# Leaky relu through an SBUF tile in six of nine chunks, one transfer for two heads' decay rows, and stores issued by ScalarE

## The chip, the cores and the metric

The kernel runs on one core of a Trainium2 chip. A core has a matrix engine (TensorE, PE in the profile; PEld is its weight load), a vector engine (VectorE, DVE), an activation engine (ScalarE, ACT), a general engine (GpSimd, POOL), and a sequencer that here issues every transfer (SyncE, SP; SPq in the rows). Each works through its own list of instructions in the order written at build time, and waits at an instruction until what it needs is there. The metric is the device time of one execution in microseconds, as the median of three runs.

## The reference, cut to what matters

```python
scores = q @ k.T / sqrt(D)                         # 4 batches x 8 heads, 576 x 576, D = 64
scores = where(causal, -1e9, scores + cum[i] - cum[j])   # cum: running sum of log(clip(f))
x   = softmax(scores) @ v                          # to 2304 tokens x 512
g   = maximum(0.01 * h, h);  h = x @ w_in          # 512 -> 2048
x   = g @ w_out                                    # 2048 -> 512
h   = x @ w_in2                                    # 512 -> 1024
ln  = layernorm(h * softmax(h)) * g_ln
out = ln @ w_out2                                  # 1024 -> 512
```

## The kernel before, in words

Every product is made with two parts per operand: a rounded high part and the rest (low part), and three matmuls high-high, high-low, low-high. So whatever feeds a matmul has first to be split by one copy (high) and one subtraction (low).

Attention runs over 16 pairs of heads in eight passes (`PASSES`, two per batch): an A pass makes query blocks 0 and 1 of four pairs, a B pass blocks 2, 3 and 4. For an A pass `prep_full` loads keys and queries into a `raw` tile of 64 rows and puts under them four rows of decay, which it reads from a DRAM tensor `dr_d` (for the first batch they lie in `qa` from the start). For a B pass `prep_split` loads a `raw` tile and splits it into `kq` tiles. Scores go to PSUM (`ps_s`), through the masked maximum (L707) and the exponential (L657) to a 16-bit tile `hl`; SP turns that with a DMA transpose into `pt` (L470), PE multiplies it with the values into `ps_v`, and `evac` brings the result into a tile `xr` (L739 on ACT, L742 on DVE). When a pair is done, `pair` stores `xr` to a DRAM tensor `xs_d`.

The first half of the feed-forward part, `ffn_a`, takes nine blocks of 256 tokens in the order `ORDER` = (0, 1, 4, 2, 5, 3, 6, 7, 8). Block n below 8 is batch n mod 4, tokens 0 to 255 or 256 to 511, so that a block can start only when a whole pass of its batch is stored: `load_x` reads the block back from `xs_d` into tiles `sd` and splits it into tiles `x`. Then `hidden` does nine of the sixteen chunks of 128 hidden columns: 12 matmuls into a PSUM tile `ps_f` (three of these exist), the leaky relu twice on ACT (L853 rounds it into the high part of `g`, L854 writes it back to PSUM), and on DVE the difference of the two as the low part (L855). The nine `g` tiles then make four partial outputs y (`ps_f<-g,wo`, 27 matmuls each), which are copied to `yo` tiles and stored to the DRAM tensor `yp_d`. The `yo` tiles are two of their own and two halves of an `sd` tile, so that rows name them either way. The tiles `x` and `g` lie where the weights were staged, so that no block starts before all 18 pieces of first-half weights are converted. Later `ffn_b` does the other seven chunks and adds the partial y back, and `layer2` does the rest.

What stands where in each engine's list is not written out by hand. Every operation is given to a planner (`Plan`) with a priority, a list of engines that may do it and a duration on each (`flex`); the planner runs through a model of the engines and puts each operation on an engine when its inputs are there and a buffer is free. So an edit at one place can move instructions everywhere. `move` takes the engines that may issue a transfer; its default is `QUEUES = ("SP",)`, and no caller names another.

Of the kernel before, what the change touches and what calls it, by code (L numbers as in the profile page):

```python
# [7 lines left out]
F32 = mybir.dt.float32  # L8
# [5 lines left out]
AF = mybir.ActivationFunctionType  # L14
# [10 lines left out]
FA = 9  # L25
PT = 4
NVT = 8
NRAW = 3
NWST = 3
NE = 2  # L30
# [327 lines left out]
def body(tc, kqa, kq, vt, f, wa, w2i, w2o, gln, out):  # L358
# [107 lines left out]
    def load(buf, dst, src, nbytes, prio, mode="w", **kw):  # L466
        return move(dst, src, nbytes, prio, **{mode: [buf]}, **kw)
# [30 lines left out]
    def row(h, p):  # L498

        return KD * h + p if p < KD else 2 * KD + (NP - KD) * h + p - KD  # L500
# [65 lines left out]
    def prep_full(p, prio):  # L566


        if p < KD:
            bq = QA[0]  # L570
            QK[p] = [[(bq, p), (bq, "n"), (bq, "c")]] * 2, lambda hd: qa[0:66, hd, p], {0: 256, 1: 384}
            return
        bq = P.buf("raw")
        a = lambda r0, r1: bq.t[r0:r1, 0:1024].rearrange("r (h c) -> r h c", h=2)
        load((bq, 0), lambda: a(0, 64), lambda: kqa[p].rearrange("(h d) c -> d h c", h=2), 64 * 1024 * 4, prio - LD)
        for hd in range(2):
            for c0, k0 in ((0, 0), (256, KB)):
                load((bq, (hd, c0)), lambda hd=hd, c0=c0: a(64, 68)[:, hd, c0:c0 + 256], lambda hd=hd, k0=k0: dr_d[row(hd, p), :, k0:k0 + 256], 4096, prio - LD,
                     deps=st["cols"])
        QK[p] = [[bq]] * 2, lambda hd: a(0, 68)[:, hd], {0: 256, 1: 384}  # L580

    def prep_split(p, prio):
# [196 lines left out]
    def pair(p, prio, blocks):  # L779
        n0 = len(P.ops)  # L780
        b, kd = divmod(p, KD)
        full = len(blocks) == 2
        (prep_full if full else prep_split)(p, prio)
        if 0 in blocks:
            prep_v(p, prio)
        xr = P.buf("xr")
        k = 0
        for hd in range(2):
            pts = {}
            for unit in UNITS[len(blocks)]:  # L790
                pts.update(scores(p, unit, hd, prio + SM + KSTEP * k, full))
                k += 1
            pv(p, hd, pts, xr, prio + AV)
            if hd == HD4 and 4 in blocks:
                pv4(p, scores4(p, prio + SM + KSTEP * k, full), xr, prio + AV)
                k += 1
        c0, c1 = 128 * blocks[0], min(S, 128 * blocks[-1] + 128)
        o = move(lambda: xs_d[b][:, kd, c0:c1], lambda: xr.t[:, c0:c1], 128 * (c1 - c0) * 4, prio - 400, r=[xr])
        spills.append((b, c0, c1, o))
        attn_ops.extend(P.ops[n0:])  # L800

# [33 lines left out]
        weight(w2o[c], W2O[c], prio, scale=lambda: glt[:, c:c + 1])  # L835


    def hidden(c, xb, n, pst, gt, prio, eprio):
        ps, g = P.buf(pst), P.buf(gt)
        w = WI[c]  # L840

        def pe():
            for k in range(KD):
                wh, wl = (w.t[:, j, 128 * k:128 * k + 128] for j in range(2))
                xh, xl = (xb[k].t[:, j, 0:n] for j in range(2))
                o = ps.t[:, 0:n]
                mm(o, wh, xh, k == 0, False)
                mm(o, wh, xl, False, False)
                mm(o, wl, xh, False, k == KD - 1)

        P.op(PE, 12 * mmr(n), pe, prio, w=[ps, (g, "slot")], r=xb + [w])
        h = lambda: ps.t[:, 0:n]
        P.op(ACT, act(n, 0, True), lambda: nc.scalar.activation(g.t[:, 0, 0:n], h(), AF.Prelu, scale=WSC, alpha=0.01), eprio, w=[(g, 0)], r=[ps])  # L853
        P.op(ACT, act(n, 0, True), lambda: nc.scalar.activation(h(), h(), AF.Prelu, scale=WSC, alpha=0.01), eprio, rw=[ps])  # L854
        P.op(DVE, dve(n) + 60, lambda: nc.vector.tensor_tensor(  # L855
            g.t[:, 1, 0:n], h(), g.t[:, 0, 0:n].bitcast(F32), op=ALU.subtract), eprio, w=[(g, 1)], r=[ps, (g, 0)])
        return g
# [33 lines left out]
    def ffn_a(blk, prio):  # L891
        eprio = prio - EP
        xb = load_x(blk, prio, "x")
        gs = [hidden(c, xb, TB, "ps_f", "g", prio + c, eprio + c) for c in range(FA)]
        YPD[blk] = []
        for d in range(KD):
            ps, yo = P.buf("ps_f"), P.buf("yo")
            for q in range(2):
                cs = range(FA // 2 * q, FA if q else FA // 2)

                def pe(cs=cs, d=d, ps=ps):
                    for c in cs:
                        y_mms(ps.t[:, 0:TB], c, d, gs[c], TB, c == 0, c == FA - 1)

                P.op(PE, 3 * len(cs) * mmr(TB), pe, prio + EPD + d, r=[gs[c] for c in cs] + [WO[c] for c in cs],
                     **({"w": [ps]} if q == 0 else {"rw": [ps]}))
            copy_f(lambda yo=yo: yo.t, lambda ps=ps: ps.t[:, 0:TB], TB, eprio + EPD + d, engs=(ACT, DVE), scale=lambda: WSC * WSC, psum=True, w=[yo], r=[ps])
            YPD[blk].append(move(lambda d=d: yp_d[blk][:, d], lambda yo=yo: yo.t, 128 * TB * 4, prio - 3000, r=[yo]))

    def ffn_b(tb, prio):  # L910
        eprio, blk = prio - 3000, ORDER[tb]
# [233 lines left out]
```

## Time and profile before

| | |
|---|---|
| runs | 846.91, 848.83, 849.77 us; median 848.83 |
| profiled execution | 848.65 us, its span 846.9 us |
| PE busy | 767.9 us, 91% |
| DVE, ACT, POOL busy | 519.4, 490.1, 348.8 us (61%, 58%, 41%) |
| DMA | 108.37 MB, mean 128 GB/s |
| chain that ended last | PE 64%, DMA 10%, DVE 9%, ACT 8% |

The shares are averages over stages that differ. The matmuls of block 0 begin at 92.4 us. From there to 391.1 us attention and `ffn_a` share PE, from 391.1 to 455.5 us `ffn_a` has PE alone, and from then on the second half runs. Busy time of PE is the time in which a matmul is under way.

### The profile page before, as it was taken

The numbers are of one execution on the slowest core, as the hardware profiler recorded it, in microseconds if no ns is written. First come the engines' busy times: TensorE is split into PE (matmuls) and PEld (weight loads), VectorE is DVE, ScalarE is ACT, GpSimd is POOL, SyncE is SP. The second block draws the span as 40 slices with busy tenths as digits, with TensorE's granted clock in tenths as the row PEclk, the third lists the DMA queues.
The fourth block names the chain that finished last, engine by engine and source line by source line (L and its number), as shares of the span: only waits on it lengthen the run. The fifth ranks groups of instructions, "written<-read, shape, count | busy, mean of one in ns | idle before, by whom it ended". The sixth has DMA issues, their size and how long they took to land.

```text
span 846.9 us, 16019 instructions
## 1 busy us (share of the span) xinstructions
PE 767.9 (91%) x5648; PEld 695.5 (82%) x5648; DVE 519.4 (61%) x1350; ACT 490.1 (58%) x1242; POOL 348.8 (41%) x448
## 2 busy tenths in 40 slices
PE   1753798979999999999899998999999999999996
PEld 1432698968998999999899987898889988998885
DVE  5788767888888878884654667334633434253551
ACT  4886768889889889884555543232333243333321
POOL 6648545166618564822610443422332233222321
PEclk9999999989999999999999999999999999999999
DMA  8997457687789677694655643321332131312223
GB/s 230 220 223 245 96 130 151 150 221 154 136 162 216 155 163 151 174 160 148 195 172 177 189 104 104 71 79 16 98 71 68 26 87 38 87 26 63 26 56 82
DMA packets 184402, 108.37 MB, mean 128 GB/s; under 512 B 150033, under 2 KB 167137, under 8 KB 184321
## 3 DMA queue, kind: packets, MB, share of 16 engines
q1 hardware_dynamic: 184320, 107.35, 52.3%
q8 instruction: 44, 0.72, 0.4%
q14 instruction: 38, 0.30, 0.1%
HBM read 57.39 MB, written 14.78 MB: 85 GB/s over the span
## 4 chain that ended last, share of the span: by engine, by line
PE 64%; DMA 10%; DVE 9%; ACT 8%; issue 4%; POOL 3%; SPq 0%; ACTq 0%; DVEq 0%; POOLq 0%
PE ps_f L473 40%; PE ph L473 10%; PE py L473 6%; PE ps_s L473 5%; PE ps_v L473 3%; ACT ps_s L657 2%; DMA raw<-w2o 2%; DMA tr<-hl 2%; DMA raw<-kq 2%; DMA wst<-wa 1%; DMA pt<-hl 1%; ACT hl L427 1%; DVE hl L438 1%; DMA qa<-sd 1%; DVE ps_s L707 1%
## 5 line engine op out<-in xcount | busy, mean ns | idle before, releaser
L473 PE MATMUL ps_f<-x,wi 128*128 128x256 f32 x972 | 131.7, 289 | 1.2 <-POOL x L442 1.1
L473 PE MATMUL ps_f<-g,wo 128*128 128x256 f32 x972 | 126.4, 284 | 2.5 <-DVE g L855 2.5
L473 PEld LDWEIGHTS ps_f<-x,wi 128*128 128x128 f32 x972 | 124.7, 193 | 3.1 <-POOL x L442 1.9
L473 PEld LDWEIGHTS ps_f<-g,wo 128*128 128x128 f32 x972 | 120.8, 188 | 4.0 <-DVE g L855 2.9
L473 PE MATMUL ph<-wi,g 128*128 128x512 f32 x408 | 98.5, 397 | 1.4 <-DVE raw L968 1.4
L473 PE MATMUL ps_f<-x,wib 128*128 128x256 f32 x756 | 97.3, 279 | 1.8 <-DVE g L855 1.7
L438 DVE SCALAR_TENSOR_TENSOR hl<-ps_s,st,hl 128x512 f16<-128x512 f32 (+4 forms) x160 | 82.8, 540 | 19.4 <-ACT hl L427 16.5
L473 PEld LDWEIGHTS ps_f<-x,wib 128*128 128x128 f32 x756 | 91.6, 188 | 2.9 <-DVE g L855 2.8
L473 PEld LDWEIGHTS ph<-wi,g 128*128 128x128 f32 x408 | 75.9, 188 | 19.3 <-DVE raw L968 1.6
L855 DVE TENSOR_TENSOR g<-ps_f,g 128x256 fp32r<-128x256 f32 x144 | 60.3, 420 | 48.1 <-ACT ps_f L854 47.2
L853 ACT ACTIVATE g<-ps_f 128x256 fp32r<-128x256 f32 x144 | 54.8, 380 | 59.3 <-PE ps_f L473 58.1
L657 ACT ACTIVATE ps_s<-ps_s,st 128x512 f32<-128x512 f32 (+4 forms) x160 | 78.6, 491 | 10.1 <-DVE st L707 6.1
L473 PE MATMUL ps_f<-wo,x 128*128 128x512 f32 x348 | 84.0, 396 | 0.0
L427 ACT ACTIVATE hl<-ps_s,st 128x512 f16<-128x512 f32 (+4 forms) x151 | 76.1, 532 | 11.6 <-DMA pt<-hl 4.7
L473 PE MATMUL ps_v<-pt,VT 128*128 128x128 f16 (+1 forms) x928 | 62.3, 220 | 20.0 <-DVE xr L742 9.0
L473 PE MATMUL py<-g,wob 128*128 128x256 f32 x567 | 75.6, 278 | 2.0 <-ACT g L427 2.0
L473 PEld LDWEIGHTS ps_f<-wo,x 128*128 128x128 f32 x348 | 64.8, 188 | 15.1
L473 PE MATMUL ps_s<-kq 128*128 128x512 f32 (+5 forms) x256 | 66.7, 380 | 11.6 <-DVE hl L438 5.5
L442 POOL TENSOR_TENSOR kq<-raw,kq 64x576 fp32r<-64x576 f32 (+1 forms) x53 | 67.9, 1283 | 21.5 <-ACT kq L427 15.2
L473 PEld LDWEIGHTS <-VT 128*128 128x128 f16 x928 | 50.0, 102 | 30.4 <-issue 15.4
L473 PEld LDWEIGHTS py<-g,wob 128*128 128x128 f32 x567 | 71.2, 188 | 4.3 <-ACT g L427 2.3
L707 DVE CUSTOM_DVE_ANT_0 ps_s<-ps_s,mask 128x256 f32<-128x256 f32 (+3 forms) x128 | 62.2, 496 | 5.9 <-PE ps_s L473 4.5
(159 smaller groups left out, 1221.7 us busy)
## 6 DMA issues: line engine op xcount, KB each, us to landing
wst<-wa SPq DMA_DIRECT2D x18, 512.0 KB
sd<-xs_d SPq DMA_DIRECT2D x32, 256.0 KB
raw<-kq SPq DMA_DIRECT2D x16, 480.0 KB
raw<-wa SPq DMA_DIRECT2D x14, 512.0 KB
raw<-yp_d SPq DMA_DIRECT2D x18, 256.0 KB
vr<-vt SPq DMA_DIRECT2D x13, 320.0 KB
raw<-w2i SPq DMA_DIRECT2D x8, 512.0 KB
raw<-w2o SPq DMA_DIRECT2D x8, 512.0 KB
```

The source lines that it names most:

```text
L427: nc.scalar.activation(o, i, CP, scale=1.0 if scale is None else scale)
L438: nc.vector.scalar_tensor_tensor(o, a, scale, b, op0=ALU.mult, op1=ALU.subtract)
L442: (nc.vector if eng == DVE else nc.gpsimd).tensor_tensor(o, a, b, op=ALU.subtract)
L473: nc.tensor.matmul(o, lhsT=l, rhs=r, start=start, stop=stop)
L657: P.op(ACT, act(W, 1, True) + 93, lambda view=view, j=j, k=k: nc.scalar.activation(view(), view(), AF.Exp, bias=sts.t[:, j:j + 1], scale=- ...
L707: P.op(DVE, dve(W) + 130, lambda i=i, j=j, view=view: nc.vector.tensor_tensor_reduce(view(), view(), mask[:, 512 - 128 * i:640], -0.125, 3 ...
L853: P.op(ACT, act(n, 0, True), lambda: nc.scalar.activation(g.t[:, 0, 0:n], h(), AF.Prelu, scale=WSC, alpha=0.01), eprio, w=[(g, 0)], r=[ps])
L855: P.op(DVE, dve(n) + 60, lambda: nc.vector.tensor_tensor(g.t[:, 1, 0:n], h(), g.t[:, 0, 0:n].bitcast(F32), op=ALU.subtract), eprio, w=[(g, ...
```

## The change

Three edits. First, the decay rows of both heads of a pair come in one transfer: two transfers of 8 KB per pair and A pass instead of four of 4 KB. Second, the stores of `xr` (32) and of the partial y (36) are given to ACT alone. Third, `hidden` has a second form, used in chunks 0 to 5 of the first seven blocks, 42 of the 81 chunks of `ffn_a`: ACT makes the leaky relu once, from PSUM into a `yo` tile; DVE or POOL copies that into the high part, and DVE or POOL subtracts for the low part. The tile `yo` is the one that the partial y also use; there are still four.

```diff
+GC, GB = (0, 1, 2, 3, 4, 5), 7
...
-        for hd in range(2):
-            for c0, k0 in ((0, 0), (256, KB)):
-                load((bq, (hd, c0)), lambda hd=hd, c0=c0: a(64, 68)[:, hd, c0:c0 + 256], lambda hd=hd, k0=k0: dr_d[row(hd, p), :, k0:k0 + 256], 4096, prio - LD,
-                     deps=st["cols"])
+        for c0, k0 in ((0, 0), (256, KB)):
+            load((bq, c0 + 1), lambda c0=c0: a(64, 68)[:, :, c0:c0 + 256], lambda k0=k0: dr_d[row(0, p):row(1, p) + 1:row(1, p) - row(0, p), :, k0:k0 + 256].rearrange("h r c -> r h c"),
+                 8192, prio - LD, deps=st["cols"])
...
-        o = move(lambda: xs_d[b][:, kd, c0:c1], lambda: xr.t[:, c0:c1], 128 * (c1 - c0) * 4, prio - 400, r=[xr])
+        o = move(lambda: xs_d[b][:, kd, c0:c1], lambda: xr.t[:, c0:c1], 128 * (c1 - c0) * 4, prio - 400, r=[xr], engs=("ACT",))
...
-    def hidden(c, xb, n, pst, gt, prio, eprio):
+    def hidden(c, xb, n, pst, gt, prio, eprio, apart=False):
...
+        if apart:
+            r = P.buf("yo")
+            P.op(ACT, act(n, 0, True), lambda: nc.scalar.activation(r.t, h(), AF.Prelu, scale=WSC, alpha=0.01), eprio, w=[r], r=[ps])
+            copy_f(lambda: g.t[:, 0], lambda: r.t, n, eprio, engs=(DVE, POOL), w=[(g, 0)], r=[r])
+            sub_f(lambda: g.t[:, 1], lambda: r.t, lambda: g.t[:, 0].bitcast(F32), n, eprio, w=[(g, 1)], r=[r, (g, 0)])
+            return g
...
-        gs = [hidden(c, xb, TB, "ps_f", "g", prio + c, eprio + c) for c in range(FA)]
+        gs = [hidden(c, xb, TB, "ps_f", "g", prio + c, eprio + c, c in GC and ORDER.index(blk) < GB) for c in range(FA)]
...
-            YPD[blk].append(move(lambda d=d: yp_d[blk][:, d], lambda yo=yo: yo.t, 128 * TB * 4, prio - 3000, r=[yo]))
+            YPD[blk].append(move(lambda d=d: yp_d[blk][:, d], lambda yo=yo: yo.t, 128 * TB * 4, prio - 3000, r=[yo], engs=("ACT",)))
```

The planner makes new lists from this. Two places matter below. The first is SP's list where the third block in the order (block 4) is read back; `sd<-xs_d` are its two loads, `xs_d_91<-xr` the last store before them, `raw<-kq` loads of the next B pass. Before:

```order
L470 DMA_TRANSPOSE pt_139<-hl_136 128x6x128
L470 DMA_TRANSPOSE pt_140<-hl_134 128x6x128
L464 DMA yp_d_96<-yo_736 128x256
L464 DMA xs_d_91<-xr_142 128x320
L464 DMA raw_81<-kq 128x960
L464 DMA vr_108<-vt 128x640
L464 DMA yp_d_96<-yo_737 128x256
L464 DMA raw_82<-kq 128x960
L464 DMA sd_85<-xs_d_91 128x2x256
L464 DMA sd_84<-xs_d_91 128x2x256
```

The same place of SP's list now:

```order
L466 DMA raw_82<-kqa 64x2x512
L466 DMA raw_82<-dr_d 4x2x256 x2
L466 DMA raw_83<-kq 128x960
L472 DMA_TRANSPOSE pt_137<-hl_134 128x6x128
L472 DMA_TRANSPOSE pt_138<-hl_135 128x6x128
L466 DMA vr_108<-vt 128x640
L472 DMA_TRANSPOSE pt_139<-hl_136 128x6x128
L466 DMA sd_85<-xs_d_91 128x2x256
L466 DMA sd_84<-xs_d_91 128x2x256
L472 DMA_TRANSPOSE pt_140<-hl_134 128x6x128
L466 DMA raw_81<-kq 128x960
```

The stores are gone from it, and one of the `kq` loads that stood ahead of the read-back now stands behind it. The store has gone to ACT's list, four rows behind the copy that fills `xr`:

```order
L429 ACTIVATE sd_86<-ps_f_163 128x256
L429 ACTIVATE hl_134<-ps_s_169,st_133 128x256
L466 DMA yp_d_96<-sd_86 128x256
L740 ACTIVATE xr_142<-ps_v_173,u_120 64x256
L429 ACTIVATE hl_135<-ps_s_171,st_129 128x256
L658 ACTIVATE ps_s_170,st_130<-ps_s_170,st_130 128x256
L658 ACTIVATE ps_s_172,st_131<-ps_s_172,st_131 128x128
L466 DMA xs_d_91<-xr_142 128x320
```

Here ACT does three other instructions before it comes to the store. The second place is PE's list where attention ends (`ps_v<-pt` is the last pair's product with the values, `ps_f<-g,wo` partial y, `ps_f<-x,wi` the first chunk of block 7). Before:

```order
L473 MATMUL ps_v_173<-pt_139,VT_116 128x128
L473 MATMUL ps_f_163<-g_731,wo_76 128x256 x3
L473 MATMUL ps_f_163<-g_732,wo_77 128x256 x3
L473 MATMUL ps_f_163<-g_733,wo_78 128x256 x3
L473 MATMUL ps_f_163<-g_734,wo_79 128x256 x3
L473 MATMUL ps_f_163<-g_735,wo_80 128x256 x3
```

These five rows are the first of 28, 84 matmuls in all, that stand there before the first `ps_f<-x,wi`. The same place now:

```order
L475 MATMUL ps_v_173<-pt_139,VT_116 128x128
L475 MATMUL ps_f_165<-x_771,wi_63 128x256 x3
L475 MATMUL ps_f_165<-x_772,wi_63 128x256 x3
L475 MATMUL ps_f_165<-x_773,wi_63 128x256 x3
L475 MATMUL ps_f_165<-x_774,wi_63 128x256 x3
```

The 84 matmuls have moved to earlier places in the list, and block 7 follows the last product directly. At the start of block 4 the count goes the other way: between the last product of the B pass that the block needs and the block's first matmul, PE's list had 30 matmuls of partial y, and now has 54.

## Rows read from the trace of the kernel before

**Rows 1.** Windows by stage: us, busy time per engine, clock, DMA share, GB/s.
```profile
0.00:92.40 92.40, 39.43 (x142) 27.18 (x143) 67.36 (x207) 64.65 (x170) 59.33 (x72) 1.00 0.83 220
92.40:391.10 298.70, 286.81 (x2616) 269.60 (x2617) 239.65 (x758) 255.11 (x703) 150.07 (x183) 0.98 0.72 158
391.10:455.50 64.40, 62.07 (x518) 61.86 (x517) 32.48 (x54) 33.10 (x77) 21.27 (x26) 1.00 0.61 190
```

**Rows 2.** Waits of PE before 100 us: us in total, times, longest.
```profile
PE ps_s L473 <- DMA raw<-dr_d: 6.2, 1, 6.2
```

**Rows 3.** Timeline, the first matmuls of block 0: start, us, engine, instruction.
```profile
92.41 2.91 PE L473 MATMUL ps_f<-x,wi 128*128 128x256 f32 x12
```

**Rows 4.** Windows of 5 us around the read-back of block 4.
```profile
175.00:180.00 5.00, 4.45 (x38) 4.00 (x38) 3.27 (x11) 3.99 (x11) 2.44 (x3) 1.00 1.01 254
180.00:185.00 5.00, 1.65 (x10) 0.98 (x10) 4.69 (x15) 3.44 (x10) 4.59 (x6) 0.86 0.96 358
185.00:190.00 5.00, 3.39 (x19) 2.64 (x18) 4.60 (x21) 4.92 (x17) 3.79 (x7) 0.50 0.82 162
190.00:195.00 5.00, 4.96 (x26) 4.21 (x25) 3.71 (x8) 4.52 (x13) 3.60 (x4) 0.62 0.53 152
```

**Rows 5.** Timeline there: start, us, engine, instruction, idle before and releaser.
```profile
174.13 2.56 SPq L470 DMA_TRANSPOSE pt<-hl  x2
174.31 0.49 DVE L742 SCALAR_TENSOR_TENSOR xr<-ps_v,u,xr 64x256 f32<-64x256 f32 x1
...
177.36 0.44 SPq L464 DMA_DIRECT2D xs_d<-xr  x1
177.40 0.98 POOL L434 TENSOR_SCALAR kq<-raw 64x960 fp32r<-64x960 f32 x1 [5.02 <-DMA raw<-kq]
...
179.05 1.66 DVE L442 TENSOR_TENSOR kq<-raw,kq 64x384 fp32r<-64x384 f32 x1
...
180.67 0.96 SPq L464 DMA_DIRECT2D sd<-xs_d  x2
...
182.98 0.49 PE L473 MATMUL ps_v<-pt,VT 128*128 128x128 f16 x6 [3.53 <-DVE xr L742]
...
189.55 2.71 PE L473 MATMUL ps_f<-x,wi 128*128 128x256 f32 x8 [1.12 <-POOL x L442]
```

**Rows 6.** Waits of SP's queue, 92 to 392 us.
```profile
SPq L464 <- DVE xr L742: 4.4, 3, 2.0
SPq L464 <- ACT yo L427: 3.1, 4, 1.2
```

**Rows 7.** Timeline at the end of attention.
```profile
390.15 0.95 PE L473 MATMUL ps_v<-pt,VT 128*128 128x128 f16 x14
390.91 10.32 PE L473 MATMUL ps_f<-g,wo 128*128 128x256 f32 x84
...
391.64 0.49 DVE L742 SCALAR_TENSOR_TENSOR xr<-ps_v,u,xr 64x256 f32<-64x256 f32 x1 [1.58 <-ACT xr L739]
...
393.76 0.97 SPq L464 DMA_DIRECT2D sd<-xs_d  x2
...
396.63 0.42 ACT L427 ACTIVATE x<-sd 128x256 fp32r<-128x256 f32 x1 [0.89 <-DMA sd<-xs_d]
...
397.39 2.31 POOL L442 TENSOR_TENSOR x<-sd,x 128x256 fp32r<-128x256 f32 x3
```

**Rows 8.** Groups by line: count, busy us, mean ns, idle before.
```profile
L855 DVE TENSOR_TENSOR g<-ps_f,g 128x256 fp32r<-128x256 f32 x144 | 60.3, 420 | 48.1 <-ACT ps_f L854 47.2
L854 ACT ACTIVATE ps_f<-ps_f 128x256 f32<-128x256 f32 x144 | 54.8, 380 | 0.1
L442 POOL TENSOR_TENSOR x<-sd,x 128x256 fp32r<-128x256 f32 x48 | 35.8, 767 | 6.2 <-ACT x L427 3.1 <-DVE x L430 1.1 <-DVE s L967 0.8
```

**Rows 9.** Issue of a partial y's store on SP: ns min/median/max.
```profile
L464 SPq DMA_DIRECT2D yp_d<-yo x18: 319/334/535, 124.9 to 456.1; - x18
```

**Rows 10.** Waits of PE, 75 to 475 us.
```profile
PE ps_f L473 <- DVE g L855: 2.5, 2, 2.3
```

## The prediction

> **What bounds the kernel now.** I read the windows by stage first [rows 1]. The reader is to see three things in them. Until 92.4 us PE is busy for 39.4 us only, while ACT, DVE and POOL are busy for two thirds of the time and the DMA engines for 0.83. From 92.4 to 391.1 us PE is busy for 286.8 of 298.7 us: 11.9 us are idle. From 391.1 to 455.5 it is busy for 62.1 of 64.4 us. So after 92.4 us PE is the bound, and an edit that changes no matmul can take away only PE's waits, or add some; ahead of that it can shift the start. The number of matmuls stays, so the time is worked out as the profiled execution's own 848.65 us, minus the waits that go, plus those that come. That is 0.18 us below the median of the three runs, 848.83 us; what I compare with is the median, and 0.3% of it, 2.55 us, is about what a measurement of this kernel can tell from no change.
>
> Next come the waits of PE. The largest hole after 92.4 us lies where block 4 is read back [rows 4]: between 175 and 190 us PE is busy for 4.45 + 1.65 + 3.39 = 9.49 us, idle for 5.5. Behind it the granted clock goes to its lower level, 1.2 instead of 2.4 GHz: the mean is 0.86, 0.50 and 0.62 in the next three windows, which is the lower level for shares of 0.28, 1 and 0.76. Half of PE's busy time in these shares is lost: 1.65 x 0.28 / 2 + 3.39 / 2 + 4.96 x 0.76 / 2 = 3.8 us. The timeline says why [rows 5]. DVE has finished the block's last `xr` at 174.80, but SP is in two transposes until 176.69, then in a store of y, and issues the `xs_d` store at 177.36, 2.56 us late. The loads of the block are issued at 180.67, behind two more `kq` loads. Meanwhile DVE and POOL are in the split of a `kq` tile that landed late (POOL stood 5.02 us for it), so that PE waits 3.53 us for a DVE evacuation, and then for the split of the block's `x`, until 189.55.
>
> **The change part by part.** *The decay rows.* 24 issues of 48 leave SP's list. In the first stage PE once waits 6.2 us for such a transfer [rows 2]. Block 0, whose matmuls begin at 92.41 [rows 3], waits for the converted weights, so that what attention wins ahead of it is worth 0 to 6.2 us at the end. I take 3.0, the middle, since the row says what is waited for there but not what comes next: the weights, whose loads stand in the same list of SP and move up a little as well.
>
> *The stores.* On SP 68 issues go. Seven blocks' y (28) and at most 28 of the `xr` stores fall between 92.4 and 391.1 us. SP stood 4.4 + 3.1 = 7.5 us in this stretch waiting for what such stores read [rows 6], with transposes and loads queued behind. For the hole at block 4 the sum is: the store no longer stands behind the transposes, 2.5 us; PE's list has 24 more matmuls of y between the last product and the block, at 10.32 / 84 = 0.123 us each [rows 7] 2.95 us, less 0.5 us for one product group (the 0.49 us row in [rows 5]) that has gone from there. Together 4.9 of the 5.5 us; bounds are 0 (POOL and DVE split `x` no sooner) and 5.5. If the hole shrinks to half a microsecond the clock has no reason to fall: 3.8 us, or 0. Of the other 11.9 - 5.5 = 6.4 us idle in the stretch I take 2.0, bounds 0 and 6.4, because the 7.5 us on SP are spread over more waiters than PE.
>
> ACT pays for the stores. Its trace has no issue of a transfer; the nearest rows are the same stores on SP: 0.33 us median for y [rows 9], 0.44 for `xs_d` [rows 5]. From above I bound it by such a store plus one transpose of SP, 2.56 / 2 = 1.28 us [rows 5], if ACT's issue had to stand behind it: 0.33 + 1.28 = 1.61. I take 0.4, the rows of the same instruction. ACT then has 56 x 0.4 = 22.4 us more and 42 x 0.380 = 16.0 less [rows 8], 6.4 net, in a stretch where it is idle for 298.7 - 255.1 = 43.6. That is cover enough, so this costs nothing on PE. If the cover is gone (a rival) it decides. Behind an ACT store that waits for DVE's half of `evac` stand the exponentials and high parts of the next units; at the place shown three ACT instructions lie between, so that the wait is short.
>
> The Trainium skill says something against this edit (Perfetto Trace Analysis, section DMA Instruction — HWDGE (DVE, Sync)): descriptor generation is one block that the two issuing sequencers share and lock, and an instruction's span holds the wait for that lock. By it ACT would often stand behind SP's transposes, and the price would go towards the 1.61 us; by the rows of SP alone it is 0.33 to 0.44. No run here shows which holds.
>
> *The leaky relu.* Chunks in the old form cost ACT twice 0.38 and DVE 0.420 us; in the new one ACT once, and a copy and a subtraction from SBUF. The new lists put almost all 42 subtractions on POOL, 0.767 us each [rows 8], about 32 us; POOL is busy for 150.1 of 298.7 us there [rows 1], so this is hidden by PE's work on other chunks. What it saves on DVE, 42 x 0.42 = 17.6 us, the planner gives back to DVE as parts of `kq` and `x`. The PSUM tile is free after one ACT instruction instead of three, but PE waited only 2.5 us in 400 for such a tile [rows 10]: 0 to 2.3, counted in the 2.0 above.
>
> *What comes.* In PE's new list the 84 matmuls behind the last product are gone, and block 7 stands there at once. It needs that product, evacuated, stored, read back and split. [Rows 7] has that chain: the product ends at 390.15 + 0.95 = 391.10, DVE at 392.13, the loads are issued at 393.76, land at 396.6, and POOL's third subtraction ends at 397.39 + 2.31 = 399.70. Before, 84 matmuls (10.3 us) covered all of it. Now the first chunk's last three matmuls end at 399.70 + 3 x 0.123 = 400.07 instead of 391.10 + 12 x 0.123 = 392.58: 7.5 us. If the split went to three engines at once, it would end about 1.5 us sooner: 6.0. A hole of this length is larger than the one that was followed by the lower clock [rows 4]; that lasted about 10 us, of which some 6 would here lie under matmuls: 3.0 us, bounds 0 and 5.1 (half of 10.2).
>
> The sum: 848.65 - 3.0 - 4.9 - 3.8 - 2.0 + 7.5 + 3.0 = 845.45 us. All gains at their upper bound and the losses at their lower give 848.65 - 6.2 - 5.5 - 3.8 - 6.4 + 6.0 = 832.8; the other way round it is 848.65 + 7.5 + 5.1 = 861.3.
>
> **The rivals.** *The hole at the end is all that is new, and the one at block 4 stays.* For it: at block 4 the split of `x`, not the store, may end last (PE waits for POOL at 189.55 [rows 5]), and POOL gets 32 us of subtractions. Against it: one `kq` split fewer stands ahead. Then 848.65 + 7.5 + 3.0 = 859.2 us. It decides as soon as less than 10.5 us of waits go elsewhere.
>
> *ACT becomes the bound.* 43.6 + 16.0 = 59.6 us of free time over 56 issues: from 1.06 us each on, ACT ends later than PE. At 1.61 us it is 56 x 1.61 = 90 us, 30 too many; moved copies (some 15 leave ACT in the new lists) take off perhaps 10: 848.65 + 20 = 868.6 us. Against it: the same stores on SP, among its transposes, took 0.32 to 0.54 us [rows 9], though from one queue.
>
> *SP's relief reaches further.* If transposes and `kq` loads come sooner all through the stretch, half of the 6.4 us and the whole of the first stage's 6.2 go too, and the new hole keeps its 7.5 without a fall of the clock: 848.65 - 6.2 - 5.5 - 3.8 - 3.2 + 7.5 = 837.5 us.
>
> *Nothing comes of it.* The waits only change place, gains 10.5 against losses 10.5: 848.6 us.
>
> **How the numbers follow.** Forecast, 845.4 us: 0.40, its own range 841 to 850, of which 0.25 is faster by over 0.3% (below 846.3), 0.14 within and 0.01 slower. The relief that reaches further, 837.5: 0.17, all faster. The hole alone, 859.2: 0.20, and ACT as the bound, 868.6: 0.11, all slower. Nothing: 0.12, of which 0.11 within and 0.01 slower. Together 0.42 faster, 0.25 the same, 0.33 slower. The range goes from 836 to 862 us: it leaves out the case of ACT and the outer part of the largest relief.
>
> **What would show it.** In the changed profile: PE's idle time around block 4's read-back (5.5 us now), and whether the granted clock still falls behind it; PE idle for 6 to 7.5 us directly behind the last `ps_v` product, with the first `ps_f<-x,wi` released by a split on POOL, and a lower clock behind that or not; the time at which block 0 starts (92.4 now); the length of ACT's transfer issues, which I put at 0.4 us. The prediction is wrong if ACT's idle time in the shared stretch goes to near nothing, if block 0 starts later than now, or if PE waits often for a low part from POOL.

## The result, and the profile after

The changed kernel takes 857.88 us (median of 4 runs, 857.21 to 858.48), the kernel before on the same chip 847.87 (845.01 to 849.77). The ratio is 1.0121, with a 95% interval of 1.0089 to 1.0153. The forecast was 845.4 us, on the other side of no change. The profiled execution took 857.21 us, its span is 855.4 us.

The windows by stage answer to [rows 1], cut at the start of block 0, the end of attention's last product and the end of the chunks of `ffn_a` (columns as there; the changed kernel's line numbers are one to seven higher than those before):

```profile
0.00:94.60 94.60, 42.03 (x159) 29.83 (x160) 77.32 (x214) 64.53 (x174) 67.20 (x83) 1.00 0.85 227
94.60:405.60 311.00, 294.77 (x2683) 277.55 (x2681) 245.28 (x741) 237.04 (x645) 180.99 (x241) 0.98 0.69 150
405.60:470.50 64.90, 55.10 (x433) 54.19 (x434) 34.35 (x60) 31.28 (x72) 22.69 (x27) 0.92 0.56 184
```

The second half begins at 470.5 us instead of 455.5, 15.0 later. PE was busy for 391.90 us until there and idle for 78.6; before it was 388.31 and 67.2. So 11.4 of the 15.0 us are idle time (4.3 more in the shared stretch, 7.5 more behind attention, 0.4 less ahead of block 0), and 3.6 us are more busy time for the same number of matmuls. The total grew by 8.5 us of span only, because the second half gave 6.5 back: its first stretch, before and then after, shows PE idle for 4.5 us and for none:

```profile
455.50:520.00 64.50, 59.97 (x454) 56.52 (x453) 43.35 (x79) 34.14 (x74) 26.82 (x32) 1.00 0.50 145
```

```profile
470.50:535.00 64.50, 64.50 (x472) 60.55 (x472) 43.88 (x81) 32.39 (x71) 25.97 (x32) 1.00 0.48 145
```

Around block 4's read-back the windows of 5 us answer to [rows 4]:

```profile
175.00:180.00 5.00, 3.77 (x36) 3.53 (x35) 4.89 (x13) 3.54 (x13) 4.46 (x4) 1.00 0.83 252
180.00:185.00 5.00, 2.72 (x22) 2.26 (x21) 4.81 (x22) 4.02 (x11) 4.81 (x8) 0.69 0.93 262
185.00:190.00 5.00, 5.00 (x30) 4.76 (x30) 4.86 (x10) 2.75 (x12) 2.76 (x3) 0.63 0.94 241
190.00:195.00 5.00, 3.84 (x31) 3.09 (x28) 3.62 (x13) 4.35 (x15) 2.46 (x5) 1.00 0.40 95
```

The hole is still there: 20 - 15.33 = 4.7 us idle, against 20 - 14.45 = 5.5 before, and the clock still falls behind it. While PE idles, DVE and POOL are full (4.8 to 4.9 and 4.5 to 4.8 of 5 us); ACT, which got the stores, is not. The timeline there answers to [rows 5]:

```profile
171.36 0.49 DVE L743 SCALAR_TENSOR_TENSOR xr<-ps_v,u,xr 64x256 f32<-64x256 f32 x1
171.88 0.33 ACTq L466 DMA_DIRECT2D xs_d<-xr  x1
...
176.50 1.10 SPq L466 DMA_DIRECT2D sd<-xs_d  x2
...
183.83 0.80 PE L475 MATMUL ps_v<-pt,VT 128*128 128x128 f16 x6 [1.82 <-DVE xr L743]
184.39 2.91 PE L475 MATMUL ps_f<-x,wi 128*128 128x256 f32 x12
```

The store leaves as soon as DVE has finished, and block 4 begins at 184.39 without a wait (before at 187.87, and it then waited for POOL until 189.55). What PE waits for in the hole now are three evacuations of attention by DVE, for 1.23, 0.46 and 1.82 us. The end of attention, in the timeline, answers to [rows 7]:

```profile
404.62 0.96 PE L475 MATMUL ps_v<-pt,VT 128*128 128x128 f16 x14 [0.70 <-DMA pt<-hl]
...
406.11 0.49 DVE L743 SCALAR_TENSOR_TENSOR xr<-ps_v,u,xr 64x256 f32<-64x256 f32 x1 [2.75 <-ACT xr L740]
406.63 0.33 ACTq L466 DMA_DIRECT2D xs_d<-xr  x1
...
409.56 0.58 PE L475 MATMUL ps_f<-x,wi 128*128 128x256 f32 x1 [3.98 <-ACT x L429]
...
411.53 2.28 POOL L444 TENSOR_TENSOR x<-sd,x 128x256 fp32r<-128x256 f32 x3
...
413.17 6.32 PE L475 MATMUL ps_f<-x,wi 128*128 128x256 f32 x35 [3.03 <-POOL x L444]
```

Here the chain is the one that the prediction priced: product, evacuation, store at once on ACT, read-back, POOL's third subtraction, and 3.98 + 3.03 = 7.0 us of PE in two waits. The windows show what the clock did behind it, mean 0.72, 0.50 and 0.76:

```profile
405.00:410.00 5.00, 1.02 (x12) 0.69 (x9) 1.18 (x2) 1.43 (x3) 1.30 (x2) 0.72 0.26 79
410.00:415.00 5.00, 1.97 (x9) 1.83 (x9) 0.91 (x2) 1.51 (x3) 3.72 (x5) 0.50 0.80 264
415.00:420.00 5.00, 4.48 (x29) 4.28 (x27) 2.89 (x4) 2.31 (x5) 3.91 (x4) 0.76 0.68 178
```

The issues of the stores on ACT answer to [rows 9] (ns min, median, max; first and last start):

```profile
L466 ACTq DMA_DIRECT2D xs_d<-xr x32: 325/326/372, 38.2 to 406.6; - x32
L466 ACTq DMA_DIRECT2D yp_d<-sd x19: 326/327/530, 129.8 to 471.1; - x19
L466 ACTq DMA_DIRECT2D yp_d<-yo x17: 326/326/1474, 121.4 to 469.3; - x17
```

Four of the waits of PE between 94 and 406 us have grown: for DVE's evacuation and for DVE's low part of `hl` (before, in its stretch, 5.4 and 1.9 us), and for SP's transposes of `hl` and for ACT's part of the values (neither is in the list of waits before):

```profile
PE ps_v L475 <- DVE xr L743: 6.3, 6, 1.8
PE ps_s L475 <- DVE hl L440: 3.8, 8, 1.1
PE ps_v L475 <- DMA pt<-hl: 3.2, 6, 1.0
PE ps_f L475 <- ACT VT L620: 2.0, 3, 0.9
```

One way in which attention comes late on DVE is to be seen at 258 us: DVE does parts of the next `kq` tile for 2.59 + 1.76 us in a row, with the reciprocal that the exponentials' next step needs behind them in its list, and ACT waits 3.01 us for it:

```profile
258.03 2.59 DVE L432 CAST kq<-kq 64x384 fp32r<-64x384 f32 x2
...
260.54 1.76 DVE L444 TENSOR_TENSOR kq<-raw,kq 64x384 fp32r<-64x384 f32 x1
...
263.38 0.15 DVE L676 RECIPROCAL st<-st 128x2 f32<-128x2 f32 x1
...
263.56 0.37 ACT L429 ACTIVATE hl<-ps_s,st 128x128 f16<-128x128 f32 x1 [3.01 <-DVE st L676]
```

Of the parts of `kq` DVE does 53 now, 33 before. In the whole shared stretch ACT waited for that reciprocal (us in total, times, longest), before and then after:

```profile
ACT hl L427 <- DVE st L675: 1.0, 2, 0.8
```

```profile
ACT hl L429 <- DVE st L676: 8.5, 10, 3.0
```

That this wait is what makes attention late is not shown: e14 below is late with 2.1 us of it.

### The profile page after: what moved, and what is told of

Same layout as the page of the kernel before. It is cut to its first block, busy times and chain, and to the rows that moved or that the text cites. A ratio compares the mean times of both kernels' runs of the same rounds, so it can differ in the third digit from the quotient of the medians.

```text
span 855.4 us, 15952 instructions
## 1 busy us (share of the span) xinstructions
PE 770.0 (90%) x5648; PEld 698.1 (82%) x5648; DVE 533.4 (62%) x1342; ACT 468.7 (55%) x1183; POOL 387.3 (45%) x516
## 4 chain that ended last, share of the span: by engine, by line
PE 59%; DMA 6%; DVE 6%; ACT 3%; issue 2%; POOL 2%; SPq 0%; POOLq 0%; DVEq 0%; ACTq 0%
PE ps_f L475 34%; PE ph L475 11%; PE py L475 8%; PE ps_s L475 3%; PE ps_v L475 2%; DMA pt<-hl 1%; DMA sd<-xs_d 1%; DMA tr<-hl 1%; DVE kq L432 1%; DVE hl L440 1%; DMA xs_d<-xr 1%; DVE ps_s L708 1%; DMA raw<-kq 1%; ACT hl L429 1%; SPq L466 0%
## 5 line engine op out<-in xcount | busy, mean ns | idle before, releaser
L475 PE MATMUL ps_f<-g,wo 128*128 128x256 f32 x972 | 129.0, 286 | 1.0 <-DVE g L862 1.0
L658 ACT ACTIVATE ps_s<-ps_s,st 128x512 f32<-128x512 f32 (+4 forms) x160 | 78.6, 491 | 10.3 <-DVE st L708 5.7
L860 ACT ACTIVATE g<-ps_f 128x256 fp32r<-128x256 f32 x102 | 38.7, 380 | 57.3 <-PE ps_f L475 56.6
L444 POOL TENSOR_TENSOR kq<-raw,kq 64x576 fp32r<-64x576 f32 (+1 forms) x48 | 62.9, 1312 | 8.6 <-ACT kq L429 2.7
L475 PEld LDWEIGHTS ps_s<-kq 128*128 128x128 f32 (+1 forms) x256 | 41.7, 199 | 27.3 <-DVE hl L440 20.1
```

What stands on the lines that cost most here:

```text
L444: (nc.vector if eng == DVE else nc.gpsimd).tensor_tensor(o, a, b, op=ALU.subtract)
L475: nc.tensor.matmul(o, lhsT=l, rhs=r, start=start, stop=stop)
L658: P.op(ACT, act(W, 1, True) + 93, lambda view=view, j=j, k=k: nc.scalar.activation(view(), view(), AF.Exp, bias=sts.t[:, j:j + 1], scale=- ...
```

## The experiments

Sixteen kernels, each timed in five rounds against the kernel before. Three theories compete at first. *L*: the leaky relu's copies and subtractions load POOL and DVE and bring attention late. *S*: the stores on ACT, or what the planner makes of them, open the hole. *D*: the decay transfers move the start. A fourth, *N*, came up with e4: no edit costs anything, but each makes the planner draw new lists for all engines, and the lists of before are a better draw than most. The table has all results. "Lists" are the order and the engine of every instruction; the last two columns are from the profiled execution, the start of attention's last product and of the second half's first matmul (us). It is one execution of each kernel, from 2.1 us below its median (e2) to 4.2 above (e11, e15), so that these two columns are good to a few us only.

| run | edits on the chip | lists | median us | ratio, 95% | last product | 2nd half |
|---|---|---|---|---|---|---|
| before | none | before | 847.5 to 848.7 | 1 | 390.9 | 455.5 |
| changed | all three | new | 857.88 | 1.0121 (1.0089 to 1.0153) | 405.4 | 470.5 |
| e1 | leaky relu | new | 853.59 | 1.0075 (1.0045 to 1.0105) | 396.8 | 461.2 |
| e2 | stores | new | 869.37 | 1.0254 (1.0226 to 1.0283) | 410.7 | 477.7 |
| e3 | decay rows | new | 857.43 | 1.0114 (1.0089 to 1.0139) | 394.1 | 461.6 |
| e4 | stores | before | 845.75 | 0.9972 (0.9953 to 0.9992) | 390.3 | 453.8 |
| e5 | none | new | 855.29 | 1.0096 (1.0066 to 1.0127) | 399.8 | 467.1 |
| e6 | none | new | 865.69 | 1.0220 (1.0188 to 1.0253) | 400.1 | 468.5 |
| e7 | leaky relu, one tile | before | 852.05 | 1.0054 (1.0030 to 1.0078) | 398.8 | 463.2 |
| e8 | stores, decay rows | before | 845.88 | 0.9980 (0.9960 to 1.0000) | 391.4 | 454.8 |
| e9 | leaky relu, two tiles | before | 847.23 | 0.9984 (0.9966 to 1.0002) | 389.1 | 454.2 |
| e10 | leaky relu | of changed | 866.50 | 1.0197 (1.0166 to 1.0229) | 414.0 | 479.6 |
| e11 | all three | of changed, y held | 862.01 | 1.0167 (1.0140 to 1.0194) | 405.8 | 472.9 |
| e12 | all three | new | 869.26 | 1.0243 (1.0218 to 1.0267) | 411.9 | 478.1 |
| e13 | all three | before | 845.04 | 0.9957 (0.9934 to 0.9981) | 388.8 | 452.4 |
| e14 | none | new order, engines of before | 864.26 | 1.0196 (1.0169 to 1.0223) | 401.6 | 466.2 |
| e15 | all three | new | 852.08 | 1.0043 (1.0020 to 1.0066) | 393.5 | 461.1 |
| e16 | stores, decay rows | new | 845.46 | 0.9977 (0.9953 to 1.0002) | 390.8 | 453.9 |

### e1 to e3: one edit each, planned anew

e1 undoes the other two edits, e2 and e3 likewise; the text of each edit is as in the diff of the change.

> Only the leaky relu's second form (42 of 81 chunks); decay rows and stores as before. In PE's list 69 matmuls of partial y stand behind the last product (84 before, 0 in the changed kernel). Theory L (POOL and DVE, loaded by copies and subtractions that ACT had, bring attention late): most of the loss is here, 853 to 858 us, ratio 1.006 to 1.012, and PE waits for kq or x of POOL and DVE. Theory S (the stores on ACT moved the y matmuls and left the end of attention open): the hole at the end is 1 to 2 us as before, 846 to 850 us, ratio 0.998 to 1.003.

> Only the stores given to ACT; decay rows and leaky relu as before. In PE's list no matmul of y stands behind the last product. Theory S: the whole hole is here, PE idle for 6 to 8 us behind the last product and a clock of 0.5 for some 10 us, 854 to 858 us, ratio 1.007 to 1.012. Theory L: a hole is there but attention ends some us earlier than in the changed kernel, since POOL and DVE are free, 848 to 851 us, ratio 1.000 to 1.004.

> Only the decay rows in one transfer for both heads. Theory D (the 2.2 us later start of block 0 comes from this edit, since PE's list now has 72 instead of 60 products ahead of it): first matmul of block 0 at 94 to 95 us, 849 to 852 us, ratio 1.001 to 1.005; 54 matmuls of y stay behind the last product, so no hole at the end. Against D (it comes from the other two edits): block 0 starts at 92.4 us or earlier, 845 to 848 us.

Each edit alone is slower, by 0.75, 2.54 and 1.14%. L's number came out for e1, D's direction for e3 (block 0 at 93.6 us, though the time is 5.4 us above D's upper bound), and e2 is 11 us beyond S's range. The three add up to 4.4%, where together they cost 1.2%. Prices that belonged to edits would not behave so: two of them would have to be undone by the third.

### e4: the stores on ACT in the lists of before

```diff
-        return flex(engs, [d[e] for e in engs], lambda e: queue[e].dma_start(dst(), src()), prio, dma=nbytes / 360.0, **kw)
+        return flex(engs, [d[e] for e in engs], lambda e: queue[by or e].dma_start(dst(), src()), prio, dma=nbytes / 360.0, **kw)
...
-        o = move(..., prio - 400, r=[xr])
+        o = move(..., prio - 400, r=[xr], by="ACT")
```

> The lists of the kernel before, with its 68 stores of x and of partial y issued by ACT at the place in time where the plan had SP issue them: nothing else moves. Theory S in the form that the planner's new lists cost the time: within 0.3% of the kernel before, 845 to 850 us, or better by the hole at block 4. Rival (the issue on ACT itself costs, by 0.33 us and waits in ACT's list): 851 to 856 us, PE waiting for exponentials and copies of ACT.

The planner plans the store on SP as before, and ACT issues it. The same 68 stores that cost 2.54% in new lists gain 0.28% here (0.08 to 0.47%). The rival, a price of the issue on ACT, is out.

The hole at block 4, which the stores were to close, is still there: between 175 and 190 us PE is idle for 6.0 us (5.5 before), and its two waits are those of [rows 5], 3.53 and 1.12 us there:

```profile
183.28 0.80 PE L475 MATMUL ps_v<-pt,VT 128*128 128x128 f16 x6 [4.21 <-DVE xr L744]
...
189.98 1.01 PE L475 MATMUL ps_f<-x,wi 128*128 128x256 f32 x3 [1.13 <-POOL x L444]
```

Here the store itself goes no earlier (at 177.64, since ACT's list has a `kq` copy ahead of it that waits for its load), but the loads of the read-back are issued at 179.48 instead of 180.67, and block 4 begins no sooner for it. Where the 0.28% arise is not shown.

### e5 and e6: no edit, another draw

```diff
-        d = {SP: 475.0, ACT: 490.0, POOL: 1040.0}
+        d = {SP: 480.0, ACT: 490.0, POOL: 1040.0}
```

```diff
-    return 0.833 * n + (52 if psum else 95) + 93 * extra
+    return 0.833 * n + (53 if psum else 95) + 93 * extra
```

> The kernel before, with one number of the planner changed that has no meaning on the chip: it plans 480 instead of 475 ns for an issue of SP. The same instructions in other lists (54 matmuls of y behind the last product, 44 instead of 33 kq parts on DVE). Theory N (the lists of the kernel before are a good draw among many, and any change that makes the planner draw again costs about 1%): 853 to 862 us, ratio 1.005 to 1.015, with no edit made. Theory E (the losses belong to the edits, by what they take on the engines or in the plan): 846 to 850 us, within 0.3%.

> A second draw: the planner adds 1 ns to each operation of ScalarE that reads from SBUF or PSUM, and no instruction changes. 42 matmuls of y stand behind the last product. Theory N: 851 to 862 us, ratio 1.003 to 1.015. Theory E: within 0.3% of the kernel before.

(In e6 only operations that read from PSUM get the nanosecond.) These numbers exist in the planner alone; the chip gets the same operations in other lists, some of them on another engine, and loses 0.96 and 2.20% (e6 above theory N's range). That is the size of all the losses above, so that none of e1 to e3, nor the changed kernel's own loss, can be charged to its edit by its time alone. Theory N stands, E falls.

### e7 and e9: the leaky relu in the lists of before

```diff
+        if apart:
+            one, two, three = (
+                lambda: nc.scalar.activation(r(), h(), AF.Prelu, scale=WSC, alpha=0.01),
+                lambda: nc.vector.tensor_copy(g.t[:, 0, 0:n], r()),
+                lambda: nc.gpsimd.tensor_tensor(g.t[:, 1, 0:n], r(), g.t[:, 0, 0:n].bitcast(F32), op=ALU.subtract))
+        P.op(ACT, act(n, 0, True), one, eprio, w=[(g, 0)], r=[ps])
+        P.op(ACT, act(n, 0, True), two, eprio, rw=[ps])
+        P.op(DVE, dve(n) + 60, three, eprio, w=[(g, 1)], r=[ps, (g, 0)])
```

(These are e7's lines; outside the 42 chunks `one`, `two` and `three` are the three instructions of before.)

> The lists of the kernel before, with the leaky relu's second form put in its place in 42 chunks: in the place of the first ACT instruction one ACT instruction into an SBUF tile, of the second a copy on DVE into the high part, of DVE's subtraction a subtraction on POOL. The SBUF tile is one of its own (one, since there is no room for more), not one of the four that partial y uses. Theory N (the edit itself costs nothing, its new lists do): 846 to 851 us, ratio 0.997 to 1.003. Theory L (the longer way by POOL brings g and attention's parts late): 853 to 858 us, and PE waits for g of POOL. The one tile can add waits of ACT, so that a loss of up to 3 us would not decide.

> As e7, the leaky relu's second form in the lists of the kernel before, now with two SBUF tiles in turn, so that ACT's result is never overwritten before it is split. Theory N (the second form costs nothing where the lists stay): 846 to 850 us, ratio 0.997 to 1.003; then e7's 1.0054 was the one tile. Theory L (the second form itself costs some 0.5%, because the low part now comes by way of POOL): 851 to 855 us, ratio 1.003 to 1.008, as e7.

In e7 the one tile `r` can be written again before the chunk in it is split, so that those chunks compute other values. Its 1.0054 lay between the two theories. With two tiles in turn (room for the second comes from a third `raw` tile that is 512 bytes per partition shorter) the edit gives 0.9984 (0.9966 to 1.0002), no loss, and L falls as far as the edit goes; e7's loss was that of one tile. Two things differ from the changed kernel: there 32 of the 42 copies are on POOL, and the tile is one of the four of partial y. No run here tries these two in the old lists. In the changed kernel's trace no wait of ACT is put down to a store of y or to the instructions that empty the tile, so that the shared tile is not seen to cost anything.

### e8 and e10: the cross of lists and instructions

e8 adds the decay rows' single transfer to e4. e10 is the other corner: the changed kernel's lists, with `by="SP"` on the stores and two issues in the place of each decay transfer.

> The lists of the kernel before, with the 68 stores issued by ACT at the place in time where SP stood in the plan, and the decay rows of both heads in one transfer where the first head's stood. Theory N (both edits cost nothing by themselves): 843 to 848 us, ratio 0.994 to 1.000, as the issue on ACT alone or lower. Theory D (the transfer of both heads' rows is itself slower or later): 850 to 857 us, block 0 later than 92.6 us.

> The cross to e8: the lists of the changed kernel with the stores issued by SP again, at the place in time where ACT stood in the plan, and with the decay rows in a transfer per head (two in a row). The leaky relu stays in its second form. Theory N (lists, not instructions): the loss stays, 855 to 862 us, ratio 1.009 to 1.017, with the hole behind the last product. Theory E (the instructions): 846 to 851 us.

e8 equals e4, so the decay transfers are worth nothing that can be measured. In e10 the loss stays, and grows to 1.97%, above theory N's range: on the changed kernel's lists too, the two edits together are the better choice (e10 takes both back, so it does not tell which). Both corners say that the loss is the lists'; neither says that the instructions cost anything.

### e11: the partial y held back

```diff
-                P.op(PE, 3 * len(cs) * mmr(TB), pe, prio + EPD + d, r=[...],
+                P.op(PE, 3 * len(cs) * mmr(TB), pe, prio + EPD + d, r=[...], deps=last() if blk == ORDER[6] and d else (),
```

> The changed kernel, where 81 matmuls of block 6's partial y are made to stand behind the last product, as 84 did in the kernel before; up to the first of them the lists are those of the changed kernel. Theory H (the order of y and products alone makes the hole at the end, and attention could have ended earlier): the hole of 8.5 us idle and its cold clock go, 846 to 850 us, ratio 0.998 to 1.003. Rival A (attention is late by itself, because its parts come late, and PE will now idle in front of the last products instead): 854 to 859 us, ratio 1.006 to 1.013, with 5 to 10 us of new idle time between 340 and 400 us.

This tests the prediction's own cause of the hole. `last()` is the last product. The 81 matmuls now stand where 84 stood before, and fill the hole; PE's timeline shows it:

```profile
398.07 0.94 PE L475 MATMUL ps_v<-pt,VT 128*128 128x128 f16 x14 [1.49 <-DVE xr L743]
401.95 1.14 PE L475 MATMUL ps_v<-pt,VT 128*128 128x64 f16 x18 [2.94 <-DMA pt<-hl]
404.51 1.65 PE L475 MATMUL ps_v<-pt,VT 128*128 128x128 f16 x14 [1.41 <-DVE xr L743]
405.92 10.75 PE L475 MATMUL ps_f<-g,wo 128*128 128x256 f32 x81
```

Yet the last product comes at the same time as in the changed kernel (start at 405.8 against 405.4), and idle time has gone ahead of it: 2.55 and 3.37 us in the windows 395 to 400 and 400 to 405. The two starts are not to be compared as they stand: this execution of e11 took 866.23 us, 4.2 more than its kernel's median, and was 3.8 us behind already at the place where PE's lists part. The windows from there to the end of the last product, for the changed kernel and then for e11:

```profile
391.38:405.57 14.19, 13.49 (x144) 12.97 (x142) 6.03 (x18) 7.11 (x20) 0.38 (x2) 1.00 0.56 139
```

```profile
395.17:406.16 10.99, 5.14 (x63) 4.60 (x64) 5.88 (x18) 5.57 (x15) 0.38 (x2) 0.76 0.55 139
```

PE is busy for 8.35 us less in front of the product, but the product comes only 3.2 us sooner; the other 5.15 us have become idle time. The kernel got no faster (862.01 us), and its second half is 391.5 us long again, as before. So rival A is right in the main, though the time is above its range: attention is late for the greater part by itself, and the hole is where PE runs out of other work.

### e12: the changed kernel drawn again

The edit is e5's, in the changed kernel.

> The changed kernel, with the same number without meaning as in e5: the planner takes 480 instead of 475 ns for an issue of SP. Theory N (each draw of lists has its own time, spread by 1 to 2%): any time between 848 and 872 us, but other than the changed kernel's by more than 0.3%. Theory E (the time follows the edits): 856 to 860 us, the changed kernel's.

869.26 us, with a ratio of 1.0243 where the changed kernel with the same three edits had 1.0121. N again.

### e13: all three edits in the lists of before

e4's, e8's and e9's edits together.

> All three edits in the lists of the kernel before: stores issued by ACT, both heads' decay rows in one transfer, and the leaky relu's second form in 42 chunks (copy on DVE, subtraction on POOL, two SBUF tiles of its own). Theory N: the three together cost nothing where the lists stay, 842 to 848 us, ratio 0.993 to 1.000, as e4, e8 and e9 apart. Rival I (the edits cost only together, since POOL, ACT and the transfers then meet): 852 to 860 us, as the changed kernel.

845.04 us, 0.9957 (0.9934 to 0.9981): the edits together gain 0.43%, and this kernel beats both. The windows by stage (0 to block 0, to the last product's end, to the second half) show POOL at 181.66 us in the shared stretch, as in the changed kernel (180.99), and attention early all the same. A busier POOL was not the cause:

```profile
0.00:89.60 89.60, 39.92 (x143) 27.09 (x143) 67.72 (x207) 64.78 (x170) 58.93 (x72) 1.00 0.84 227
89.60:389.00 299.40, 288.02 (x2616) 271.51 (x2617) 239.81 (x758) 245.38 (x661) 181.66 (x225) 0.97 0.72 158
389.00:452.40 63.40, 62.31 (x517) 61.90 (x516) 31.31 (x53) 32.76 (x77) 21.67 (x26) 1.00 0.61 187
```

### e14: order or choice of engines

```diff
-    def flex(engs, durs, emit, prio, **kw):
+    def flex(engs, durs, emit, prio, pin=True, **kw):
         box = []
+        if len(engs) > 1 and pin:
+            i = "ADP".index(PIN[len(PINNED)])
+            PINNED.append(i)
+            i = tuple(engs).index((ACT, DVE, POOL)[i])
+            engs, durs = engs[i:i + 1], durs[i:i + 1]
```

`PIN` holds the engine of each of the 952 choices in the kernel before.

> The instructions of the kernel before, each of the 952 that the planner could place put on the very engine that it had there (30 kq parts on ACT, 33 on DVE, 97 on POOL), and the order alone planned again. No matmul of y is left behind the last product. Theory O (the order of the lists makes attention late): 853 to 866 us, ratio 1.006 to 1.022, attention's last product at 396 us or later. Rival G (the choice of engines does, DVE having got kq parts of ACT): 846 to 851 us, last product at 390 to 393 us.

864.26 us, so the order is enough. The windows of the shared stretch and of the one behind it make it plain beside [rows 1]: DVE 240.07 us and POOL 150.06 for 239.65 and 150.07 before, the same work on the same engines. PE has 83 matmuls of y more ahead of the last product, and is idle for 15.2 and 9.4 us instead of 11.9 and 2.3:

```profile
92.10:401.80 309.70, 294.48 (x2699) 278.04 (x2699) 240.07 (x758) 256.94 (x707) 150.06 (x183) 0.99 0.71 153
401.80:466.20 64.40, 54.99 (x434) 54.02 (x434) 32.87 (x55) 31.88 (x74) 20.97 (x26) 0.95 0.61 187
```

### e15 and e16: what about the order

Products are counted here in matmuls with the values. In PE's lists of before, 60, 156, 310, 452, 548, 698 and 822 of them stand ahead of the starts of the first seven blocks; in the changed kernel's 72, 156, 304, 434, 536, 652 and 790. The planner charges ACT 490 ns for an issue and makes it wait for SP's; with 330 ns and no such wait, lists came out with attention further ahead.

```diff
-        d = {SP: 475.0, ACT: 490.0, POOL: 1040.0}
+        d = {SP: 475.0, ACT: 330.0, POOL: 1040.0}
...
-                    elif o.dma is not None and e != "POOL":
+                    elif o.dma is not None and e == "SP":
```

> The changed kernel, its planner charging ACT 330 ns for an issue (the trace shows 325 to 327 ns) without a wait for a generator shared with SP. In the lists drawn so, attention stands further ahead: 84, 234, 342, 498, 574, 730 and 868 products before the blocks' starts (72, 156, 304, 434, 536, 652 and 790 in the changed kernel; 60, 156, 310, 452, 548, 698 and 822 before). Theory C (the count of products ahead of a block is what decides, few of them make attention late): attention's last product at 380 to 392 us and 843 to 850 us in all. Rival R (the count tells nothing, a new order is late whatever its counts): last product at 396 us or later, 852 to 868 us. Rival B (blocks that start too late cost as much): last product early, yet 852 us or more, with a long hole behind it, since no y stands there.

> The stores on ACT and the decay rows without the leaky relu, in lists drawn with the same price of 330 ns: 84, 234, 328, 452, 560, 698 and 822 products before the blocks' starts, at every block as many as in the kernel before or more, and 69 matmuls of y behind the last product. Theory C: last product at 385 to 392 us, 843 to 850 us. Rival R: 396 us or later, 852 to 868 us.

e16 is as theory C has it: last product at 390.8, 845.46 us, so a new order need not be late. e15 fits none of the three: its product lies between the bounds (393.5, in an execution 4.2 us above the median), its time is 852.08 us, and it has no long hole. And e6 speaks against the count as the whole story: its counts differ from before's at one block only (666 for 698), and its last product is late by 9 us, of which 42 matmuls of y moved ahead of it make up 5.2. What in the order decides is not settled. What goes with the time over all runs is the last product: with it at 391.4 us or earlier the ratio is 0.9957 to 1, between 393.5 and 401.6 it is 1.0043 to 1.0220, from 405 on 1.0121 to 1.0254. That is no measure of attention alone, since 84 matmuls of y stand behind the product in the lists of before and 0 to 81 in the new ones, at 0.123 us each. From that product to the second half it takes 63 to 68 us more, and the second half's length varied from 385 to 396 us.

## Why the prediction was wrong

The step that failed is the first of its argument: that the time is the old execution's, minus the waits that the edits take away, plus those that they bring. It took the new lists as the old ones with two places changed. All other waits, too, were those of the old lists, and e5, e6 and e14 show that a new draw of the lists, with no edit at all, brings 0.96 to 2.20%, where the three edits in the old lists gain 0.43% (e13). By its steps:

- *Decay rows, -3.0 us.* Block 0 starts at 94.57 us, 2.2 later and not earlier. PE's 6.2 us for the transfer are gone from the waits before 100 us, but it waits there 13.3 us for DVE's `hl`, 7.4 in one piece (9.6 and 3.0 before). PE's idle time ahead of block 0 is the same, 52.6 us for 53.0; what makes the start later is 2.6 us of busy time, with 72 products instead of 60 ahead of it. In the old lists block 0 came earlier with the edit (90.3 us in e8, 92.6 in e4, one execution each; in the place of 7.4 us for the transfer PE waited 7.9 us for ACT's `kq`), but e8's time equals e4's, so that no gain of the start is seen at the end.
- *The hole at block 4, -4.9 idle and -3.8 clock.* 0.9 idle came, and by the same working of the windows 1.1 us of clock (2.7 lost instead of 3.8). The store did go at once, and block 4 began earlier, but the wait that ends last in the hole was not the store's: PE waits for DVE's evacuations, with DVE and POOL full. The first rival had it that the hole stays; its reason, POOL's split of `x`, holds in e4, where the hole is as long as before, and not in the changed kernel.
- *Other idle time, -2.0.* Between the start of block 0 and the end of the last product it rose: 16.2 - 4.7 = 11.5 us outside block 4 instead of 6.4.
- *ACT's issues, 0.4 us and hidden.* Right: 0.326 us, and ACT is idle for 74 us of the stretch. The rival of ACT as the bound is out; e4 shows that the stores on ACT cost nothing.
- *The leaky relu, 0.* Right as far as e9 goes: 0.9984 with an interval that holds 1.
- *The end of attention, +7.5 and +3.0.* The size came out: 7.5 us more idle behind the last product, and by the windows about 2.4 us of clock. The cause was mistaken for the greater part, so that the right size was in part luck. When 81 matmuls of y were held back, 5.15 of the 8.35 us taken from ahead of the last product came back as idle time there (e11). Attention ended 14.5 us later, of which 10.3 are the time of the y matmuls moved ahead of it; by e11 the greater part of these would otherwise have been idle time in front of the product.
- *What it left out.* The second half gave 6.5 us back, PE's idle time there falling from 11.8 to 6.8 us. Why is not shown.

So 859.2, the rival in which the hole at the end is all that is new, lies within 2 us of the result, but by offsetting terms: 2.2 us at the start and 4.3 more idle in the shared stretch, against 6.5 that came back. Of the prediction's own signs of being wrong one came, block 0 starting later; ACT's idle time did not go, and PE waited for no low part from POOL.

Of the 68 issues on ACT 23 began while a transpose was under way on SP's queue, and the longest of these took 372 ns; one issue of the 68 took 1474 ns. By the Trainium skill (Perfetto Trace Analysis, section DMA Instruction — HWDGE (DVE, Sync)) the issuing sequencers share one descriptor generator, which is locked for one of them at a time. The trace shows no wait of the length of a transpose in those 23 issues; the single long one may be such a wait. So neither the dear price of 1.61 us nor ACT as the bound is part of the result.

## What to carry to other kernels

Where a planner or scheduler makes the lists, an edit is two changes: the instructions, and a new draw of the order everywhere. Measure them apart, by keeping the old lists and changing only what is emitted, and by a change without meaning in the planner that shows how far draws differ; here new draws came out between 0.2% faster and 2.5% slower than the kernel before, and the edits were worth 0.4%. When a hole opens where filler work has moved away, ask first whether the awaited chain itself is late: move the filler back and look where the idle time goes, counting from a place up to which both lists agree.

## What the runs showed of the hardware that was not expected

Transfers issued by ScalarE cost it about 0.33 us each (medians 326 to 332 ns in the changed kernel, e4, e8 and e13), beside SP's transposes, which stood in SP's queue at 1.2 us each; 23 of the changed kernel's 68 began during a transpose and took 326 to 372 ns. And a loss of 2% came from order alone, with the busy time of DVE, ACT and POOL in the shared stretch unchanged to within 2 us (e14: DVE 240.07, ACT 256.94, POOL 150.06).
